# Closing the last pair of the first token block tile by tile, taking the first two tiles' scores from unsplit float32 loads, and moving the first low parts to GpSimd

## The chip, the cores and the metric

The kernel runs on one core of a Trainium2 chip. The metric is the device time of one execution in microseconds (us); three executions give the median that is compared.

## The reference, cut to what matters

Top-k attention feeds two feed-forward layers, all in float32:

```python
scores = scale * np.matmul(q, k.transpose(0, 1, 3, 2))          # (4, 8, 576, 64), scale 1/8
kth = np.partition(scores, -32, axis=-1)[..., -32:-31]
scores = np.where(scores >= kth, scores, -1e9)
attn = np.exp(scores - np.max(scores, -1, keepdims=True))
attn = attn / (np.sum(attn, -1, keepdims=True) + 1e-09)
x = np.matmul(attn, v)                                           # then (2304 tokens, 512)
h = np.maximum(x @ w_in, 0.0);   x = h * h @ w_out               # d_ff 2048
h = x @ w2_in;  out = np.maximum(0.01 * h, h) @ w2_out
```

The weights arrive as 64-bit numbers and are turned into pairs of float32 parts on the chip.

## The kernel before, in words

Queries are cut into units of 64 to 320 tokens of one batch; a unit has four head pairs (`hp`), and a unit with one head pair is a `uh`. Its queries are cut into tiles of 128 rows (two heads behind each other); two tiles make a pair (`pr`). There are 72 pairs and each pair has 16 slots of an event table: `at(slot, fn, ...)` puts a step into a slot, and the program is written out slot by slot. A scheduler then orders each engine's queue from that program with its own estimate of times; `urgent` gives a step a higher priority there, and `behind(key)` keeps an instruction after a named one. Each engine takes its own queue strictly in order, so a waiting instruction holds all behind it.

One tile goes through these steps. `load_q`, `load_k` (SP queue, DMA) bring queries and keys. `split_q`, `split_k` make a rounded high part (`split_hi`, on ACT or POOL) and a low part (a subtraction on POOL, or on DVE where `QLO_D`, `KLO_D` say so). `scores` multiplies them on PE (two products for each half of 288 keys) and ACT copies the result to `s`, scaled. DVE takes the 32 largest of a row by four MAX and three MATCH_REPLACE passes over the 576 scores, 14 passes for a pair, which are written into the first 14 slots of the pair. Then `shifts` (the difference `nb` of the 32nd and first value), `drop` and `expo_sum` (ACT: all below the 32nd go to zero, exponentials and their sum), `recip`, `pt_main` and `pt_left` (PE transposes of the probabilities `e`, copied to `PT` by ACT; also the reciprocals `rb`), `av` (product with the values) and `x_out` (DVE normalises to `xn`, ACT writes the high part `xh`, POOL or DVE the low part `xl`).

The tokens form six blocks (`BLOCKS`), the first of 512. Its attention is in the first 16 pairs (0 to 15; `first_done` is 15); only when pair 15 has given `xh` and `xl` of head pair 3 can `moe(0, 0)`, the first layer of the first block, be completed in its first products. `moe` runs 16 steps `f` for a block and layer: 12 products `h`, activation `ga`, high and low part `gh`, `gl`, 12 products `acc`. In steps met for the first time the weights are converted (`w_convert`: ACT `wc`, `att`, `wi`, `wo`; DVE bits; POOL low parts); the first two steps' weights are converted ahead by `lead_passes` and `lead_bits`. Batches 2 and 3 (`EARLY`) have their scores computed during the first 16 pairs as filler, stored to DRAM (`stage`, `sd`) and loaded later.

For pair 15 the steps stand like this, all after its 14th pass:

```python
at(z + 13, urgent(shifts), pr)
for i in range(2):
    at(z + 13, urgent(drop), pr, i)
    at(z + 13, urgent(expo_sum), pr, i)
at(z + 13, urgent(recip), pr)
for i in range(2):
    at(z + 14, urgent(pt_main), pr["t"][i])
at(z + 14, urgent(pt_left), pr)
```

When the last `x_out` of the first two units is through, `open_late` gives the SBUF of the `early` pool to the `late` one; the first `vraw` load of the later units (`load_v`, L257) goes into it, and ACT writes its high part `VT`.

## Time and profile before

| | |
|---|---|
| median of three runs | 1183.76 us (1182.36 to 1184.87) |
| the profiled execution, its own time | 1181.85 us |
| its span | 1180.1 us, 1.75 us of the time lie around it |
| PE busy | 1120.4 us (95%) |
| DVE busy | 840.8 us (71%) |
| ACT busy | 817.0 us (69%) |
| GpSimd (POOL) busy | 746.4 us (63%) |
| chain that ended last, by engine | PE 70%, ACT 10%, DVE 7%, DMA 3% |

The program has two parts. Until about 184 us DVE makes the top-k passes of the first 16 pairs while PE, ACT and POOL do the other steps and the filler; after that the feed-forward products keep PE busy to the end, with the attention of the later units beside them.

### The profile page before, as it was taken

To read this page: it belongs to the slowest core of one execution; us is meant where nothing else is said; L and a number is where in the kernel's file an instruction comes from. 1 tells how busy PE (TensorE), PEld (TensorE's weight loads), DVE (VectorE), ACT (ScalarE), POOL (GpSimd) and SP (SyncE) were. 2 spreads that over 40 slices of the span, in tenths; PEclk is the share of its full clock that TensorE was granted. 3 is DMA by queue.
4 is the path that set the end of the run, shared out by engine and by line. 5 is a ranking of instruction groups with operands and counts; after the bars stand their busy time and mean duration, and the time that the engine had idled before them with its cause. 6 is when DMAs were issued, how large, how long until landed. Compare 5 with 4: busy or idle time off the path is not lost.

```text
span 1180.1 us, 20025 instructions
## 1 busy us (share of the span) xinstructions
PE 1120.4 (95%) x6376; PEld 984.7 (83%) x6376; DVE 840.8 (71%) x1771; ACT 817.0 (69%) x1823; POOL 746.4 (63%) x960
## 2 busy tenths in 40 slices
PE   5898978899899999999999999999999999999998
PEld 4777766687678899989999998888788899999997
DVE  7999998867675669999999999989999200110011
ACT  6899997999889778877677677556866633333322
POOL 7968837899878767667898776767756543002100
PEclk9899988999999999999999999999999999999999
DMA  9768766999999588899988888667676489779974
GB/s 305 271 211 285 252 223 220 376 344 326 341 339 363 213 325 287 274 308 373 328 284 297 300 273 306 227 209 236 228 229 205 156 319 341 258 249 355 345 256 135
DMA packets 108201, 329.53 MB, mean 279 GB/s; under 512 B 17216, under 2 KB 25408, under 8 KB 104000
## 3 DMA queue, kind: packets, MB, share of 16 engines
q1 hardware_dynamic: 105472, 323.53, 79.3%
q10 hardware_dynamic: 2624, 4.72, 1.1%
q8 instruction: 52, 0.85, 0.3%
q14 instruction: 53, 0.43, 0.1%
HBM read 257.03 MB, written 71.17 MB: 278 GB/s over the span
## 4 chain that ended last, share of the span: by engine, by line
PE 70%; ACT 10%; DVE 7%; DMA 3%; issue 2%; POOL 2%; ACTq 0%; SPq 0%; POOLq 0%; DVEq 0%
PE h L653 28%; PE acc L692 15%; PE acc L690 13%; PE att L447 4%; DVE m L932 4%; PE att L350 3%; DVE w L934 3%; PE att L436 2%; ACT stage L311 1%; ACT e L333 1%; PE att L310 1%; PE sp L310 1%; ACT e L329 1%; ACT s L311 1%; DMA vraw<-in_v_dram 1%
## 5 line engine op out<-in xcount | busy, mean ns | idle before, releaser
L653 PE MATMUL h<-xh,wi 128*128 128x512 f32 (+2 forms) x1280 | 346.4, 343 | 8.8 <-ACT xh L704 3.5
L932 DVE MAX8 m<-w 128x8 f32<-128x576 f32 x432 | 311.1, 747 | 2.2
L653 PEld LDWEIGHTS h<-xh,wi 128*128 128x128 f32 x1280 | 226.1, 189 | 34.9 <-ACT ga L670 4.8
L673 POOL TENSOR_TENSOR gl<-ga,gh 128x512 fp32r<-128x512 f32 (+2 forms) x160 | 162.3, 1017 | 126.6 <-ACT gh L672 108.6
L934 DVE MATCH_REPLACE8 w<-m,w 128x576 f32<-128x576 f32 x288 | 213.0, 742 | 0.6
L653 PE MATMUL h<-xl,wi 128*128 128x512 f32 (+2 forms) x640 | 204.5, 339 | 0.0
L358 POOL TENSOR_TENSOR PTs<-whole,PTs 128x512 fp32r<-128x512 f32 x112 | 144.5, 1297 | 43.3 <-ACT whole L357 39.8
L690 PE MATMUL acc<-gh,wo 128*128 128x512 f32 (+2 forms) x768 | 157.0, 343 | 0.9 <-ACT gh L664 0.9
L692 PE MATMUL acc<-wo,gh 128*128 128x512 f32 x576 | 153.2, 397 | 0.2 <-ACT gh L672 0.2
L690 PEld LDWEIGHTS acc<-gh,wo 128*128 128x128 f32 x768 | 127.1, 190 | 13.1 <-ACT gh L664 1.7
L653 PEld LDWEIGHTS h<-xl,wi 128*128 128x128 f32 x640 | 120.3, 190 | 10.7
L329 ACT ACTIVATE e<-s,m 128x576 f32<-128x576 f32 x144 | 112.2, 782 | 24.1 <-DVE m L932 16.2
L932 DVE MAX8 m<-s 128x8 f32<-128x576 f32 x144 | 104.4, 748 | 30.3 <-ACT s L311 26.3
L673 DVE TENSOR_TENSOR gl<-ga,gh 128x384 fp32r<-128x384 f32 x32 | 17.9, 559 | 151.2 <-ACT gh L672 148.5
L670 ACT ACTIVATE ga<-h 128x512 f32<-128x512 f32 (+2 forms) x96 | 46.4, 489 | 114.1 <-PE h L653 112.1
L692 PEld LDWEIGHTS acc<-wo,gh 128*128 128x128 f32 x576 | 104.6, 188 | 20.0 <-ACT gh L672 0.4
L333 ACT ACTIVATE e<-e,nb 128x576 f32<-128x576 f32 x144 | 111.3, 778 | 4.8 <-POOL nb L323 4.7
L934 DVE MATCH_REPLACE8 w<-m,s 128x576 f32<-128x576 f32 x144 | 106.8, 743 | 0.3
L350 PE MATMUL att<-ident,e 128*128 128x128 f32 x576 | 88.5, 277 | 7.4 <-ACT e L333 6.7
L665 POOL TENSOR_TENSOR ga<-ga 128x512 f32<-128x512 f32 (+2 forms) x80 | 66.1, 828 | 44.0 <-ACT gh L664 41.6
L345 POOL TENSOR_SCALAR e<-e,rc 128x576 f32<-128x576 f32 x112 | 82.6, 748 | 11.5 <-DVE rc L341 10.9
L447 PE MATMUL att<-PTs,VT 128*128 128x256 f32 (+2 forms) x504 | 86.9, 297 | 2.0 <-ACT whole L357 1.7
(101 smaller groups left out, 2065.6 us busy)
## 6 DMA issues: line engine op xcount, KB each, us to landing
wi<-wd SPq DMA_DIRECT2D x160, 512.0 KB, 5.2
wo<-wd SPq DMA_DIRECT2D x160, 512.0 KB, 5.1
wraw<-in_w_dram SPq DMA_DIRECT2D x32, 1024.0 KB, 8.2
sd<-stage SPq DMA_DIRECT2D x76, 288.0 KB, 3.2
s<-sd SPq DMA_DIRECT2D x76, 288.0 KB, 5.0
wd<-wi SPq DMA_DIRECT2D x32, 512.0 KB, 7.4
wd<-wo SPq DMA_DIRECT2D x32, 512.0 KB, 7.3
vd<-VT SPq DMA_DIRECT2D x16, 640.0 KB, 6.3
```

Of the source, the lines that this page charges most:

```text
L329: ACT.activation(t["e"], t["s"], AF.Prelu, bias=pr["m8"][:, i, 31:32], scale=-1.0, alpha=1.0 / FAR)
L333: ACT.activation(e, e, AF.Exp, bias=pr["nb"][:, i:i + 1], scale=-FAR, accum_out=pr["sum"][:, i:i + 1])
L345: POOL.tensor_scalar(e, e, pr["rc"][:, i:i + 1], 1.0, op0=OP.mult, op1=OP.mult)
L350: PE.transpose(ps[:, j * P:(j + 1) * P], t["e"][:, j * P:(j + 1) * P], ident)
L358: POOL.tensor_tensor(pts[:, 4:8, c:c + P], whole, pts.bitcast(F)[:, 0:4, c:c + P], op=OP.subtract)
L447: PE.matmul(ps, lhsT=l, rhs=r, start=i == 0, stop=i == len(mm) - 1)
L653: PE.matmul(two[r][:, 0:n], lhsT=ws[r][:, w, c * P:(c + 1) * P], rhs=x[c][y][:, 0:n], start=cnt == mine[0], stop=cnt == mine[-1])
L673: (DVE if j >= GLD else POOL).tensor_tensor(gl[:, 0:n], a[:, 0:n], gh.bitcast(F)[:, 0:n], op=OP.subtract)
L690: PE.matmul(acc[c][:, 0:n], lhsT=wo[:, w, cs], rhs=g[:, 0:n], start=first, stop=last)
L692: PE.matmul(acc[c], lhsT=g[:, cs], rhs=wo[:, w, :], start=first, stop=last)
L932: cur["dve"] = DVE.max(out=m8[:, x, 8 * r:8 * r + 8], in_=t["s"] if r == 0 else t["w"])
L934: cur["dve"] = DVE.match_replace(out=t["w"], in_to_replace=m8[:, x, 8 * r:8 * r + 8], in_values=t["s"] if r == 0 else t["w"], imm_value=NEG)
```

## The change

Seven things change.

1. The first `uh`: its queries and keys are loaded in three DMAs each, first the 64 rows of head 0 (L288, L236), then their copy in the lower 64 partitions (L294, L242), then head 1 (L295, L243). The copy exists because the low part is made there.
2. Tiles 0 and 1 take their scores from these unsplit 64 rows as whole float32, one product for each half instead of two (L318), and are `urgent`. The split parts are still made, for tiles 2 and 3 of the same `uh`.
3. `KLO_D` and `QLO_D` are empty: the first queries' and keys' low parts go from DVE to POOL.
4. Pair 15: its passes are written one tile after the other, and `close` does everything for one tile as soon as that tile's seven passes are done. The first pass of the tiles of pair 16 stays behind the `nb` of the second close.
5. Pair 14: its closing steps are urgent, a few slots earlier, with `nb` on DVE and the sum on ACT.
6. The first two steps' weights: the sign now comes through ACT's Prelu, so DVE's second pass (L591) goes; the steps go half by half.
7. The conversion of the third step's weights starts behind the last `xh` of pair 15.

```diff
-KLO_D = ((0, 0), (0, 1))
-QLO_D = (0,)
+KLO_D = ()
+QLO_D = ()
...
+        if st["i"] == 0:
+            SP.dma_start(st["k"][0:D, 0], k[b, hp, 0:D, 0])
+            cur["k"] = st["k"]
+            return
         SP.dma_start(st["k"], k[b, hp])
+
+    def load_k_rest(b, hp, st):
+        SP.dma_start(st["k"][D:P, 0], k[b, hp, D:P, 0])
+        SP.dma_start(st["k"][:, 1], k[b, hp, :, 1])
...
+        if uh["idx"] == 0:
+            SP.dma_start(t[0:D, 0, 0:n], q[0, 0, 0:D, 0, 0:n])
+            return
...
+    def load_q_rest(uh):
+        n = uh["n"]
+        SP.dma_start(uh["q"][D:P, 0, 0:n], q[0, 0, D:P, 0, 0:n])
+        SP.dma_start(uh["q"][:, 1, 0:n], q[0, 0, :, 1, 0:n])
...
-        mm = [(x[:, h, c:c + P], kt[:, h, ks]) for h, c in t["parts"] for x in d]
+        mm = [(uh["q"][0:D, 0, t["i"] * P:t["i"] * P + P], cur["k"][0:D, 0, ks])] if t["i"] < 2 else [(x[:, h, c:c + P], kt[:, h, ks]) for h, c in t["parts"] for x in d]
...
-        on = DVE if pr["p"] == first_done else POOL
+        on = DVE if pr["p"] == first_done - 1 else POOL
...
+    def close(pr, i):
+        t, uh, m = pr["t"][i], pr["t"][i]["uh"], slice(i, i + 1)
+        if i == 0:
+            pr["nb"] = pool.tile([P, 2], F, tag="nb", name="nb", bufs=2)
+        cur["shift"] = DVE.tensor_tensor(pr["nb"][:, m], pr["m8"][:, i, 31:32], pr["m8"][:, i, 0:1], op=OP.subtract)
+        drop(pr, i)
+        expo_sum(pr, i)
+        ACT.activation(pr["sum"][:, m], pr["sum"][:, m], AF.Copy, bias=1e-9)
+        cur["recip"] = DVE.reciprocal(pr["rc"][:, m], pr["sum"][:, m])
+        pt_main(t)
+        ps = stage_psum.tile([P, 512], F, tag="sp", name="sp", bufs=SPB)
+        c, r0 = t["col"], (t["i"] - uh["ti"]) * P - uh["n"]
+        PE.transpose(ps[0:LEFT, 0:P], t["e"][:, NJ * P:S], ident)
+        ACT.activation(PT[0:64, 4, c:c + P], ps[0:64, 0:P], AF.Copy)
+        PE.transpose(ps[:, P:2 * P], pr["rc"][:, m].to_broadcast([P, P]), ident)
+        if "rb" not in uh:
+            uh["rb"] = early.tile([P, 256], F, tag="rb", name="rb", bufs=2)
+        ACT.activation(uh["rb"][D:2 * D, r0:r0 + P], ps[D:2 * D, P:2 * P], AF.Copy)
...
-            ACT.activation(b, raw[:, :, 0], AF.Copy, scale=L_SCALE, bias=L_BIAS)
+            with behind("closed") if i == 2 else ExitStack():
+                ACT.activation(b, raw[:, :, 0], AF.Copy, scale=L_SCALE, bias=L_BIAS)
...
-            ACT.activation(v, hi.bitcast(F), AF.Copy, scale=H_SCALE)
+            ACT.activation(v, hi.bitcast(F), AF.Prelu, scale=H_SCALE, alpha=2.0 ** 32)
...
-                DVE.scalar_tensor_tensor(b, vu, 0x80000000, b, op0=OP.bitwise_and, op1=OP.bitwise_or)
...
-            at(z + 13, urgent(shifts), pr)
...
+                at(z + 6 + 7 * i, urgent(close), pr, i)
...
-            z = 16 * (uh["lastA"] // 2 if hs == (0,) else uh["last"] // 2) + (15 if near else 27 if tight and apart else 30)
+            z = 16 * (uh["lastA"] // 2 if hs == (0,) else uh["last"] // 2) + (15 if near else 23 if tight and apart else 30)
...
+            if p == first_done:
+                x, r, top = i // 7, i % 7 // 2, i % 7 % 2 == 0
...
+                with behind("shift") if p == first_done + 1 and r == 0 else ExitStack():
+                    cur["dve"] = DVE.max(out=m8[:, x, 8 * r:8 * r + 8], in_=t["s"] if r == 0 else t["w"])
```

Since the scheduler orders the queues anew, they differ from the start to about the first third of PE's program; behind that (from about 420 us of the trace before) PE's queue is the same instruction for instruction.

SP's queue at the start of the program, before; `qraw_148` and `kraw_151` belong to the first `uh`, `qraw_157` to the second, `qraw_170` to the third, `qraw_224`, `qraw_226` and `kraw_230` to the filler:

```order
L279 DMA qraw_148<-in_q_dram 128x2x256
L235 DMA kraw_151<-in_k_dram 128x1152
L279 DMA qraw_157<-in_q_dram 128x2x256
L279 DMA qraw_224<-in_q_dram 128x2x256
L279 DMA qraw_226<-in_q_dram 128x2x320
L235 DMA kraw_230<-in_k_dram 128x1152
L279 DMA qraw_170<-in_q_dram 128x2x256
```

The same after (the second `uh` is now `qraw_161`, the third `qraw_174`):

```order
L288 DMA qraw_148<-in_q_dram 64x256
L294 DMA qraw_148<-in_q_dram 64x256
L290 DMA qraw_161<-in_q_dram 128x2x256
L236 DMA kraw_151<-in_k_dram 64x576
L242 DMA kraw_151<-in_k_dram 64x576
L243 DMA kraw_151<-in_k_dram 128x576
L295 DMA qraw_148<-in_q_dram 128x256
L290 DMA qraw_224<-in_q_dram 128x2x256
L290 DMA qraw_226<-in_q_dram 128x2x320
L290 DMA qraw_174<-in_q_dram 128x2x256
L239 DMA kraw_230<-in_k_dram 128x1152
```

The first keys stand fourth instead of second, the filler's keys behind the third `uh`'s queries, and that load waits for POOL's second low part of `qraw_161`.

ACT's queue at the start, before; `s0_101` and `s1_102` are the scores of tiles 0 and 1:

```order
L129 ACT_TABLE_LOAD
L129 ACTIVATE q00_77<-qraw_148 128x256 x2
L129 ACTIVATE KT_150<-kraw_151 128x576 x2
L129 ACTIVATE q01_83<-qraw_157 128x256 x2
L311 ACTIVATE s0_101<-sd_179 128x288
L311 ACTIVATE s0_101<-sd_172 128x288
L311 ACTIVATE s1_102<-sd_183 128x288
L311 ACTIVATE s1_102<-sd_187 128x288
L129 ACTIVATE q00_77<-qraw_170 128x256
```

The same after:

```order
L129 ACT_TABLE_LOAD
L129 ACTIVATE q00_77<-qraw_148 128x256
L129 ACTIVATE q01_83<-qraw_161 128x256 x2
L129 ACTIVATE KT_150<-kraw_151 128x576
L327 ACTIVATE s0_101<-sd_176 128x288
L129 ACTIVATE KT_150<-kraw_151 128x576
L129 ACTIVATE q00_77<-qraw_148 128x256
L327 ACTIVATE s0_101<-sd_182 128x288
L327 ACTIVATE s1_102<-sd_185 128x288
L129 ACTIVATE q00_77<-qraw_174 128x256
L327 ACTIVATE s1_102<-sd_188 128x288
```

The copies of the first scores are now mixed with the splits of the first `uh` and of the third; a wait for the load L294 stands ahead of the table load.

DVE's queue from the middle of the closing of pair 15 to its last low part `xl_672`, before (`m_2506` are the maxima of pair 16):

```order
L934 MATCH_REPLACE w<-m_2506,s_104 128x576
L591 SCALAR_TENSOR_TENSOR wc<-v,wc 128x512
L467 TENSOR_TENSOR xn<-att,rb 64x256
L591 SCALAR_TENSOR_TENSOR wc<-v,wc 128x512
L932 MAX m_2506<-w 128x8 x2
L934 MATCH_REPLACE w<-m_2506,w 128x576
L467 TENSOR_TENSOR xn<-att,rb 64x256
L932 MAX m_2506<-w 128x8
L472 TENSOR_TENSOR xl_672<-xn,xh_671 64x256
```

The same after (`m_2508` are the maxima of pair 16, `m_2777` those of pair 17):

```order
L502 TENSOR_TENSOR xn<-att,rb 64x256
L974 MATCH_REPLACE w<-m_2508,w 128x576
L972 MAX m_2508<-w 128x8
L972 MAX m_2508<-s_104 128x8
L974 MATCH_REPLACE w<-m_2508,s_104 128x576
L972 MAX m_2508<-w 128x8
L974 MATCH_REPLACE w<-m_2508,w 128x576
L972 MAX m_2508<-w 128x8
L972 MAX m_2777<-s_105 128x8
L502 TENSOR_TENSOR xn<-att,rb 64x256
```

Eight passes now stand between the two `xn`, three before; after them three more passes and `xl_672` follow.

ACT's queue from the last `xh` of pair 15 to the first activation `ga`, before:

```order
L468 ACTIVATE xh_671<-xn 64x256
L543 ACTIVATE wc<-wraw 128x1024
L329 ACTIVATE e_108<-s_104,m_2506 128x576
L333 ACTIVATE e_107,sum<-e_107,nb 128x576
L311 ACTIVATE s_105<-att 128x288
L129 ACTIVATE VT<-vraw 128x5x64 x2
L311 ACTIVATE s_106<-att 128x288
L333 ACTIVATE e_108,sum<-e_108,nb 128x576
L129 ACTIVATE q_77<-qraw 128x256
L311 ACTIVATE s_106<-att 128x288
L663 ACTIVATE ga<-h 128x512 x2
```

The same after:

```order
L503 ACTIVATE xh_671<-xn 64x256
L581 ACTIVATE wc<-wraw 128x1024
L590 ACTIVATE att<-wraw 128x512
L581 ACTIVATE wc<-wraw 128x1024
L327 ACTIVATE s_101<-att 128x288
L345 ACTIVATE e_108<-s_104,m_2508 128x576
L349 ACTIVATE e_107,sum<-e_107,nb 128x576
L601 ACTIVATE wi<-wc 128x512
L590 ACTIVATE att<-wraw 128x512
L349 ACTIVATE e_108,sum<-e_108,nb 128x576
L701 ACTIVATE ga<-h 128x512 x2
```

`VT` has gone behind `ga`, and the conversions of the third and fourth step's weights have come ahead of it.

## Rows read from the trace of the kernel before

**Rows 1.** The page: the span, and DVE's busy share in 40 equal slices (tenths).

```profile
span 1180.1 us, 20025 instructions
...
DVE  7999998867675669999999999989999200110011
```

**Rows 2.** Windows: us, busy time (instructions) by engine, clock, DMA share, GB/s.

```profile
190.00:200.00 10.00, 6.11 (x19) 4.59 (x19) 9.31 (x20) 9.22 (x22) 8.11 (x10) 0.71 0.67 222
200.00:240.00 40.00, 36.22 (x166) 28.74 (x165) 32.30 (x63) 36.35 (x69) 35.43 (x38) 0.99 1.00 361
240.00:300.00 60.00, 57.21 (x275) 46.97 (x276) 38.83 (x73) 55.12 (x103) 59.66 (x58) 1.00 0.95 337
```

**Rows 3.** Timeline around pair 15's closing: start, length, engine, line, operation [idle, releaser].

```profile
170.72 0.74 DVE L932 MAX8 m<-w 128x8 f32<-128x576 f32 x1
172.16 0.15 DVE L323 TENSOR_TENSOR nb<-m 128x2 f32<-128x2 f32 x1
172.23 1.28 DVE L590 SCALAR_TENSOR_TENSOR wc<-v,wc 128x512 uint32<-128x512 uint32 x2
179.70 1.12 ACT L543 ACTIVATE wc<-wraw 128x1024 uint32<-128x1024 uint32 x1
185.33 0.41 ACT L468 ACTIVATE xh<-xn 64x256 fp32r<-64x256 f32 x1
186.12 0.42 DVE L472 TENSOR_TENSOR xl<-xn,xh 64x256 fp32r<-64x256 f32 x1
190.46 0.83 ACT L129 ACTIVATE VT<-vraw 128x320 fp32r<-128x320 f32 x2 [0.31 <-DMA vraw<-in_v_dram]
192.85 1.08 ACT L663 ACTIVATE ga<-h 128x512 f32<-128x512 f32 x2
194.84 0.85 PE L310 MATMUL att<-KT,q 128*128 128x288 f32 x2 [3.66 <-ACT s L311]
195.92 3.78 PE L690 MATMUL acc<-gh,wo 128*128 128x512 f32 x8 [0.23 <-ACT gh L664]
```

**Rows 4.** The chain that ended last, in order of time: start, length, what.

```profile
244.94 2.73 PE h L653 x12
...
331.99 7.43 DMA wraw<-in_w_dram
...
581.75 2.65 DVE m L932 x4
```

**Rows 5.** Timeline of the start: columns as in rows 3.

```profile
0.73 1.28 ACT L129 ACT_TABLE_LOAD   x1 [0.73 <-PEq L995]
...
1.45 0.58 SPq L235 DMA_DIRECT2D kraw<-in_k_dram  x1
...
2.08 1.86 SPq L279 DMA_DIRECT2D qraw<-in_q_dram  x3
...
4.01 0.72 ACT L129 ACTIVATE q<-qraw 128x256 fp32r<-128x256 f32 x2 [1.99 <-DMA qraw<-in_q_dram]
...
5.63 1.26 ACT L129 ACTIVATE KT<-kraw 128x576 fp32r<-128x576 f32 x2 [0.90 <-DMA kraw<-in_k_dram]
...
7.15 1.33 PE L310 MATMUL sd<-KT,q 128*128 128x288 f32 x4 [7.15 <-DVE KT L272]
...
8.38 2.78 POOL L289 TENSOR_TENSOR q<-qraw,q 128x256 fp32r<-128x256 f32 x4
...
9.02 0.76 DVE L932 MAX8 m<-s 128x8 f32<-128x576 f32 x1 [1.25 <-ACT s L311]
...
11.22 0.69 ACT L311 ACTIVATE s<-sd 128x288 f32<-128x288 f32 x2
11.22 0.74 DVE L932 MAX8 m<-w 128x8 f32<-128x576 f32 x1
...
15.69 2.78 POOL L272 TENSOR_TENSOR KTa<-kraw,KTa 64x576 fp32r<-64x576 f32 x2
...
19.36 2.81 POOL L272 TENSOR_TENSOR KT<-kraw,KT 64x576 fp32r<-64x576 f32 x2
...
21.96 0.70 ACT L311 ACTIVATE s<-sd 128x288 f32<-128x288 f32 x2
...
23.64 0.74 DVE L932 MAX8 m<-s 128x8 f32<-128x576 f32 x1
```

**Rows 6.** DMA issues: KB each, median us from issue to landing.

```profile
qraw<-in_q_dram SPq DMA_DIRECT2D x20, 256.0 KB, 4.4
...
qraw<-in_q_dram SPq DMA_DIRECT2D x4, 64.0 KB, 2.5
```

**Rows 7.** The page's groups: busy, mean ns of one | idle before.

```profile
L333 ACT ACTIVATE e<-e,nb 128x576 f32<-128x576 f32 x144 | 111.3, 778 | 4.8 <-POOL nb L323 4.7
```

More of the change, by code (lines that the diff above doesn't have):

```diff
@@ L340, in recip @@
             POOL.tensor_scalar(pr["sum"], pr["sum"], 1e-9, 1.0, op0=OP.add, op1=OP.mult)
-        cur["recip"] = DVE.reciprocal(pr["rc"], pr["sum"])
+        DVE.reciprocal(pr["rc"], pr["sum"])
+    def close(pr, i):
[16 more added lines that the diff above has]
+        ACT.activation(uh["rb"][D:2 * D, r0:r0 + P], ps[D:2 * D, P:2 * P], AF.Copy)
     def norm(pr, i):
@@ L467, in x_out @@
             DVE.tensor_tensor(x[r, 0:n], uh["avb"][r, 0:n], uh["rb"][r, 0:n], op=OP.mult)
-        ACT.activation(xh[r, c:c + m], x[r, 0:m], AF.Copy)
+        closed = ACT.activation(xh[r, c:c + m], x[r, 0:m], AF.Copy)
         if m < n:
@@ L471, in x_out @@
         closes = uh["last"] // 2 == first_done and hs == (1,)
+        if closes:
+            cur["closed"] = closed
         (DVE if closes else POOL).tensor_tensor(xl[r, c:c + m], x[r, 0:m], xh.bitcast(F)[r, c:c + m], op=OP.subtract)
@@ L583, in lead_passes, with lead_bits @@
             ACT.activation(b, lo, AF.Copy, scale=L_SCALE, bias=L_BIAS)
-            ACT.activation(v, hi.bitcast(F), AF.Copy, scale=H_SCALE)
+            ACT.activation(v, hi.bitcast(F), AF.Prelu, scale=H_SCALE, alpha=2.0 ** 32)
             led[i].append((b, v.bitcast(U), w))
-    def lead_bits(i):
-        for b, vu, w in led.pop(i):
-            with behind("recip" if i else "shift"):
+    def lead_bits(x):
+        for i in range(2):
+            b, vu, w = led[i][x]
+            with behind("recip" if x else "shift"):
                 DVE.scalar_tensor_tensor(b, vu, 3, b, op0=OP.logical_shift_left, op1=OP.bitwise_or)
-                DVE.scalar_tensor_tensor(b, vu, 0x80000000, b, op0=OP.bitwise_and, op1=OP.bitwise_or)
             split_hi(w[:, 0, :], b.bitcast(F))
@@ L818, in topk_attention_moe_moe2_kernel @@
                 at(z - DLEAD + 2 + 5 * i, scores, t, 1)
-            at(z + 13, urgent(shifts), pr)
             for i in range(2):
-                at(z + 13, urgent(drop), pr, i)
-                at(z + 13, urgent(expo_sum), pr, i)
-            at(z + 13, urgent(recip), pr)
-            for i in range(2):
-                at(z + 14, urgent(pt_main), pr["t"][i])
-            at(z + 14, urgent(pt_left), pr)
+                at(z + 6 + 7 * i, urgent(close), pr, i)
             continue
@@ L834, in topk_attention_moe_moe2_kernel @@
             else:
-                at(z - DLEAD + 5 * i, scores, t, 0)
-                at(z - DLEAD + 2 + 5 * i, scores, t, 1)
+                mine = urgent(scores) if p == 0 else scores
+                at(z - DLEAD + 5 * i, mine, t, 0)
+                at(z - DLEAD + 2 + 5 * i, mine, t, 1)
+            soon = urgent if p == first_done - 1 else lambda fn: fn
             if i == 0:
-                at(z + 14, shifts, pr)
-            at(z + 14 + i, drop, pr, i)
-            at(z + 16 + i, expo_sum, pr, i)
+                at(z + 14, soon(shifts), pr)
+            at(z + 14 + i, soon(drop), pr, i)
+            at(z + 16 + i, soon(expo_sum), pr, i)
             if split(t["uh"]):
                 at(z + 20 + i, norm, pr, i)
-            at(max(z + 20 + 3 * i, z + 21 + i), pt_main, t)
-        at(z + 18, recip, pr)
-        at(z + 26, pt_left, pr)
+            at(z + 20 + i if p == first_done - 1 else max(z + 20 + 3 * i, z + 21 + i), soon(pt_main), t)
+        at(z + 18, soon(recip), pr)
+        at(z + 22 if p == first_done - 1 else z + 26, soon(pt_left), pr)
     rslot = [None] * len(blocks)
```

20 lines of the change are left out of this document (11 added, 9 removed).

## The prediction

> **What bounds the kernel now.** I read the page's slices first. In the first six of 40 slices (to about 177 us) DVE's digits are 7, 9, 9, 9, 9, 9 [rows 1]: there it makes the 224 passes of pairs 0 to 15. They run from 9.02 [rows 5] to the end of pair 15's last MAX, 170.72 + 0.74 = 171.46 [rows 3]: 162.4 us, 0.72 us a pass with the few other steps between. I call 171.46 T. From T the chain of waits leads through the closing of pair 15 to `moe(0, 0)`, and from about 245 us it is nearly all PE, with short stretches of DMA (331.99) and DVE (581.75) [rows 4].
>
> The timeline of the closing [rows 3] gives, counted from T: `nb` 0.7; last `xh` 13.9 (185.33); last `xl` 14.7 (186.12); `VT`, held by a DMA, 19.0 (190.46); first `ga` 21.4 (192.85); first `acc` 24.5 (195.92). PE idles 3.66 us in front of 194.84 and then makes eight `acc` products in 3.78 us, 0.47 each, where twelve `h` products later take 2.73, 0.23 each [rows 4]. In the window 190 to 200 the granted clock is 0.71, at 200 to 240 it is 0.99 [rows 2]: after the idle time PE is at the lower of its levels, 1.2 instead of 2.4 GHz. So a microsecond counts if it (a) starts DVE earlier, (b) shortens T to `ga`, or (c) fills PE's gap with products that must be made anyway.
>
> **The start (parts 1 to 3).** SP issues about 0.62 us apart (three in 1.86) and a 64 KB load lands 2.5 us after its issue, 256 KB 4.4 (median) [rows 5, 6]. The load L294 is SP's second instruction, which is issued at 1.45, and so has landed at 3.9. ACT waits for it ahead of its table load of 1.28 [rows 5], so ACT is free at 5.2 instead of 2.0. Then come, by the new queue with the row's durations (a split 0.36, a key half 0.63, a half of the scores about 0.35): 0.36 + 0.72 + 0.63 + 0.36 + 0.63 + 0.36 + 0.41 = 3.5, so the first MAX could start at 8.65 instead of 9.02. I bound it by 8.2 (L294 lands earlier) and 9.3 (it lands at 4.5). That is little, and it is not what counts: DVE has three passes on tile 0 alone and needs `s_102` for the fourth, which stood at 11.22 [rows 5]. In the new queue the second half of `s_102` is behind the split of the third `uh`'s queries; their load waits for POOL's second low part of the second `uh`. POOL makes 4 x 0.70 from 8.38 before [rows 5]; now it begins behind the first split, at 5.5, and has done three at 7.6. The first load of 256 KB takes from about 0.8 (0.62 before the 1.45 of the second) to 4.01, 3.2 us, with no other in its way; so 10.8, a split and a copy of 0.77: 11.5. The fourth pass is **0.3 us later**, not earlier; between 1.0 earlier (load under 2.5) and 1.5 later (4.4).
>
> The low parts cost POOL 2 x 0.70 + 2 x 1.39 = 4.2 us [rows 5] in front of the filler's keys; DVE loses the same pieces, but it did them while it had nothing to do, before 9.02. The second keys' low parts end at 22.17 before and feed `s_105`, used at 23.64 as the 22nd pass [rows 5]. After, I get 24.3 for the low parts' end (POOL starts earlier, so only 2.1 of the 4.2 remain), and `s_105` is now the 24th pass, at 11.5 + 20 x 0.69 = 25.3. The margin stays near 1 us: **cost 0**, and what it costs if that cover goes is rival D. PE's whole float32 products (two cold passes each) equal the split products they replace, and PE waits there anyway: 0. Four more issues on SP are 2.5 us of a queue that has free slots: 0.
>
> If the halves of a load move one after the other instead of side by side, L294 lands at 0.8 + 2 x 2.5 = 5.8, ACT is free at 7.1, the first MAX starts at 10.6 and the fourth pass at 12.7 behind three of 0.69: 1.2 later than I took. The sum below would be -1.8 instead of -3.0; the bound of 1.5 above holds it, no row of before shows a halved load, and I stay with the side-by-side value.
>
> The Trainium skill, "DMA: Bandwidth & Descriptors", section "Rules for kernel authors", states just that: two transfers to disjoint partition halves serialize, and one transfer of 128 partitions is to be used instead; by it the change's first part would cost time.
>
> **T after.** Beside the +0.3: the pass of pair 16 that stood ahead of T now stands behind it (-0.7), a second `nb` and reciprocal inside (2 x 0.15 = +0.3), gaps of less than one pass. T is unchanged, 171.5, between -1.5 and +1.5.
>
> **The closing (parts 4 to 7).** Between the last `nb` and the last `xl` the new queue of DVE has 16 passes (x 0.70 = 11.2), four steps of the weights' bits (0.64 each, half of the 1.28 in rows 3 = 2.6), two `xn` (0.42 each by the `xl` of the same shape) and a reciprocal: 14.9. So `xl` comes at T + 15.4, no earlier than T + 14.7; but the last `xn` has three passes less in front of it and the bits pass of 2.55 us (4 x 0.64, L591) is gone: 0.7 + 13 x 0.70 + 2.6 = T + 12.4, and `xh` **T + 12.9 instead of 13.9**. DVE's queue, not ACT's or PE's work on the tile, is what holds `xn`; that is why closing tile 0 seven passes early yields only one microsecond.
>
> From `xh` to `ga` ACT has, in the new order: `xh` 0.41, two `wc` 2 x 1.12 (179.70), two `att` 2 x 0.6 (half of a `wc`), `s` 0.41, a drop 0.78, `wi` 0.6, two exponentials 2 x 0.78 [rows 3, 7] = 7.2: `ga` at **T + 20.1 instead of 21.4**, 1.3 us earlier (if nothing waits for DMA: bounds 0 and 2). The load that held `VT` no longer stands in front of `ga`. In return the third step's weights are converted before it: its 12 products can be made by PE between the second step's products and the first `acc`. They are 12 x 0.23 = 2.7 us that PE needn't do later [rows 4]. PE's products of head pair 3 wait for `xl`, so of its gap I leave what I can't fill: after the 12 it has nothing from about T + 16.5 to `ga`, 3.6 us, so it idles as before and is at the lower clock behind it, as in rows 2 and 3.
>
> Against T, then: `ga` -1.3, the 12 products -2.7, and +1.0 because these twelve, and some products of later steps, run partly at the lower clock and because a step that ACT did later is now in front. Sum **-3.0** (bounds -1.5 and -4.5 with the T above). The other edits (the sum's +1e-9 on ACT, 0.2; `PT` and `rb` copied in halves; pair 14's steps, urgent) lie beside DVE's passes, which bound that stretch, so 0; without the cover each is a few tenths.
>
> **Is it kept?** From about 420 us PE's queue is the same. A lead of 3 us survives if the stretch to there isn't bound elsewhere: between 200 and 240 the DMA share is 1.00 and PE 36.2 of 40; between 240 and 300 POOL is busy 59.66 of 60 and the chain has a wait of 7.43 us for raw weights at 331.99 [rows 2, 4]. This is the weakest step. For it: the raw loads of the next steps are issued some 9 us earlier, as their buffers come free with the earlier conversion.
>
> The profiled execution took 1181.85 us, 1.9 below the median 1183.76. 1181.85 - 3.0 = 1178.85; on the median, **1180.8 us**.
>
> **The rivals.** B: the closing does what it reads like. If the scheduler's DVE queue has slack that I count as busy, the last `xh` comes at T + 10 or before, `ga` with it, and the idle 3.66 us and half of the 3.78 us behind it (1.9, products at the full clock) go as well: with rounding -6, **1178**. Against it: DVE's digits of 9 [rows 1] and 13 passes in front of `xn`.
>
> C: the lead is given back before 420 us, for POOL or the DMA decide there [rows 2]; 0, **1183.8**. For it: POOL 59.66 of 60. Against it: PE has 57.2 of 60 in that window, so POOL is not waited for at length.
>
> D, the slower side: the start starves DVE. If the third `uh`'s load takes the median 4.4 (+1.2) and POOL's 4.2 us are not absorbed, the scores `s_102` to `s_106` come late by 1.2 + 4.2 = 5.4 us in all; every microsecond in which DVE waits there moves T, and DVE has no idle time to make it up later. 5.4 less the 1.2 of the closing: +4.2, **1188**. It decides as soon as these waits exceed about 4 us in total; below that it eats the gain.
>
> That the change doesn't do what it says is part of C: DVE's queue still mixes both tiles of pair 15, so that tile 0 closes only a few passes ahead of tile 1, and `VT` behind `ga` may only move its wait.
>
> **How the numbers follow.** About 0.2%, 2.4 us, is what a measurement can tell from no change; the line lies at 1181.4. My forecast has a chance of 0.45 with its own range of 1179.3 to 1182.3 (faster 0.28, same 0.17). B 0.20, all faster. C 0.20 (same 0.18, slower 0.02). D 0.15 (slower 0.12, same 0.03). Together faster 0.48, same 0.38, slower 0.14. The range reaches from 1176.0 (B, 2 us more) to 1186.0, which leaves out the worse half of D and the far end of B.
>
> **What would show it.** First MAX near 8.7 and the fourth pass near 11.5; no idle time of DVE over 1 us between 12 and 35 us (D if there is). T near 171.5. Last `xh` about T + 13 and `ga` about T + 20 (B: `xh` by T + 10, PE without a gap over 1 us). Twelve more `h` products in front of the first `acc`, and a granted clock in that window again well below 1. From 420 us on PE's instructions shifted by one constant, 3 us; if the shift is 3 at 200 and 0 at 420, it is C. The forecast is wrong in kind if T itself moves by more than 1.5 us or if a new wait on DMA shows between `xh` and `ga`.

## The result and the profile after

The changed kernel takes 1196.16 us (median of six runs, 1191.96 to 1197.46) against 1183.8 of the kernel before: ratio 1.0104 (95% interval 1.0086 to 1.0121), 12.4 us slower. The prediction was 1180.8, range 1176.0 to 1186.0. The profiled execution took 1197.46 us; its page answers to [rows 1]:

```profile
span 1195.6 us, 20042 instructions
...
DVE  6997999776676567999999999999999300110011
```

DVE's fourth slice (about 90 to 120 us) has dropped from 9 to 7, the first from 7 to 6: DVE waits in the stretch where its passes set the time. The timeline of ACT, PE and DVE at the start (start, length, engine, line, operation, [idle before, releaser]) answers to [rows 5]:

```profile
3.69 1.28 ACT L129 ACT_TABLE_LOAD   x1 [3.69 <-DMA qraw<-in_q_dram]
6.18 4.30 PE L326 MATMUL sd<-kraw,qraw 64*128 64x288 f32 x8 [6.18 <-DMA kraw<-in_k_dram]
6.95 0.68 ACT L129 ACTIVATE KT<-kraw 128x576 fp32r<-128x576 f32 x1 [0.70 <-DMA kraw<-in_k_dram]
9.14 0.76 DVE L972 MAX8 m<-s 128x8 f32<-128x576 f32 x1 [9.14 <-ACT s L327]
12.68 0.42 ACT L129 ACTIVATE q<-qraw 128x256 fp32r<-128x256 f32 x1 [2.83 <-DMA qraw<-in_q_dram]
13.43 0.76 DVE L972 MAX8 m<-s 128x8 f32<-128x576 f32 x1 [1.88 <-ACT s L327]
```

The first pass is at 9.14 (9.02 before), the fourth at 13.43 (11.22 before). The fourth pass waits for a copy of `s_102` behind ACT's split of the third `uh`'s queries, and that split waits for their load. That is the chain of the prediction, but 1.9 us later than its 11.5.

DVE's waits between 20 us and the end of pair 15's passes, before (first fence) and after (second; what waits, for what, us in total, times, longest):

```profile
DVE m L932 <- ACT s L311: 1.1, 2, 0.8
DVE rc L341 <- POOL sum L340: 0.7, 3, 0.3
DVE m L932 <- ACT q L129: 0.6, 1, 0.6
DVE m L932 <- POOL nb L323: 0.5, 1, 0.5
```

```profile
DVE m L972 <- ACT s L327: 4.5, 3, 3.2
DVE m L972 <- POOL nb L339: 2.2, 2, 1.3
DVE rc L357 <- POOL sum L356: 1.1, 1, 1.1
DVE xn L502 <- ACT rb L436: 0.9, 2, 0.6
```

That is 2.9 us before and 8.7 after; those after all lie beyond 80 us. The last MAX of pair 15 ends at 181.12 (180.38 + 0.74) instead of 171.46 [rows 3]: 9.7 later, of which 2.2 is the fourth pass, 5.8 the growth of these waits, and 1.7 I can't assign (0.64 of it may be the `nb` of pair 14, which now takes that long on DVE at 174.44). The first `ga` follows at 204.10, 23.0 us behind that MAX (21.4 before):

```profile
180.38 0.74 DVE L972 MAX8 m<-w 128x8 f32<-128x576 f32 x1
183.89 0.76 DVE L972 MAX8 m<-s 128x8 f32<-128x576 f32 x1 [1.73 <-ACT s L327]
197.50 0.41 ACT L503 ACTIVATE xh<-xn 64x256 fp32r<-64x256 f32 x1
204.10 1.06 ACT L701 ACTIVATE ga<-h 128x512 f32<-128x512 f32 x2
204.73 0.50 PE L691 MATMUL h<-xh,wi 128*128 128x512 f32 x1 [2.27 <-ACT ga L701]
209.44 2.02 PE L728 MATMUL acc<-gh,wo 128*128 128x512 f32 x8
```

PE's idle time around `ga` is 2.27 instead of 3.66. The third step's 12 products do stand before the first `acc`, and the first eight `acc` take 2.02 us instead of the 3.78 before.

`ga` is 11.3 us late, the end of the span 15.5 (1195.6 against 1180.1). To see where the rest goes I counted ACT's copies `gh` (the high parts made from `ga`) from the program's end and compared their starts with the same copy before. The copy that stood at 238.2 us is 10.4 late, the one at 278.3 13.2, at 326.7 15.1, at 430.7 15.2, at 654.8 15.3, and the last one (1170.7) 15.8. So another 4 us are lost between about 240 and 330 us, and from there the delay is nearly constant. The first 40 us behind `ga` are not it: counted from each kernel's own `ga` they are the same before (first line) and after (second), in PE's busy time (34.19 and 34.10 us) and in the granted clock (0.91 and 0.91):

```profile
192.85:232.85 40.00, 34.19 (x142) 26.79 (x143) 35.70 (x70) 36.10 (x70) 35.01 (x36) 0.91 0.97 348
204.10:244.10 40.00, 34.10 (x143) 27.07 (x144) 29.88 (x59) 34.74 (x69) 36.92 (x39) 0.91 0.90 326
```

Behind that, the chain that ended last differs. Before, it runs from 245 to 299 us mostly through PE's products, and between 200 and 360 us through one load of raw weights (331.99, 7.43 us [rows 4]). In the changed kernel it runs through four, at 213.06, 347.10 and, where the 4 us are lost, at

```profile
290.10 7.97 DMA wraw<-in_w_dram
300.88 8.77 DMA wraw<-in_w_dram
```

That these loads make the 4 us is read from the chain; no run changes them alone, and e1, which is not late, has two such loads on its chain there (196.14 and 256.24).

Where the first of DVE's waits beyond 80 us comes from shows in POOL's and PE's rows. The first rows are of the kernel before, the second of the changed one, at the same place of the program:

```profile
79.91 1.06 PE L310 MATMUL sp<-KTa,q 128*128 128x288 f32 x6
80.81 2.52 PE L436 MATMUL att<-PT,VN 128*128 128x256 f32 x10
```

```profile
82.48 0.79 PE L326 MATMUL sp<-KTa,q 128*128 128x288 f32 x4
83.11 1.89 PE L471 MATMUL att<-PT,VN 128*128 128x256 f32 x8
...
85.78 0.53 PE L326 MATMUL sp<-KTa,q 128*128 128x288 f32 x2
86.27 0.46 POOL L131 TENSOR_SCALAR q<-qraw 128x320 fp32r<-128x320 f32 x1 [3.28 <-PE sp L326]
...
96.55 2.76 POOL L280 TENSOR_TENSOR KT<-kraw,KT 64x576 fp32r<-64x576 f32 x2
99.39 0.20 POOL L339 TENSOR_TENSOR nb<-m 128x2 f32<-128x2 f32 x1
99.62 1.42 DVE L972 MAX8 m<-s 128x8 f32<-128x576 f32 x2 [1.32 <-POOL nb L339]
```

Before, all six products of a filler step stand ahead of the ten products `att`; now two of them stand behind. POOL's next split waits 3.28 us for those two (its buffer is free only then), does the filler's keys and the direct keys behind that, comes late with `nb`, and DVE's next MAX waits for `nb`. The longest wait, 3.17 us, ends with ACT's copy of the second half of a tile's scores:

```profile
111.99 0.69 PE L326 MATMUL sd<-KT,q 128*128 128x288 f32 x4
113.64 1.01 ACT L327 ACTIVATE stage<-sp 128x288 f32<-128x288 f32 x3
114.80 0.81 ACT L345 ACTIVATE e<-s,m 128x576 f32<-128x576 f32 x1
115.47 0.44 ACT L327 ACTIVATE s<-sd 128x288 f32<-128x288 f32 x1
115.95 0.76 DVE L972 MAX8 m<-s 128x8 f32<-128x576 f32 x1 [3.17 <-ACT s L327]
```

PE has the products at 112.68, but three copies of the filler's scores (`stage`) and a drop stand ahead of that copy in ACT's queue. Both chains are read from the rows; the experiments below move whole queues and don't single any wait out.

### The profile page after: what moved, and what is told of

The parts are those of the page before. It is cut to its first block, busy times and chain, and to the rows that moved or that the text cites. A ratio compares the mean times of both kernels' runs of the same rounds, so it can differ in the third digit from the quotient of the medians.

```text
span 1195.6 us, 20042 instructions
## 1 busy us (share of the span) xinstructions
PE 1128.1 (94%) x6376; PEld 989.9 (83%) x6376; DVE 839.5 (70%) x1766; ACT 817.7 (68%) x1827; POOL 751.7 (63%) x962
## 4 chain that ended last, share of the span: by engine, by line
PE 64%; ACT 8%; DVE 5%; DMA 4%; issue 2%; POOL 1%; ACTq 0%; SPq 0%; DVEq 0%; POOLq 0%
PE h L691 28%; PE acc L730 15%; PE acc L728 11%; PE att L482 4%; PE att L385 3%; DMA wraw<-in_w_dram 3%; DVE m L972 2%; DVE w L974 2%; PE att L326 1%; ACT wc L581 1%; ACT e L349 1%; ACT att L590 1%; PE att L400 1%; ACT e L345 1%; DMA wi<-wd 1%
## 5 line engine op out<-in xcount | busy, mean ns | idle before, releaser
L728 PEld LDWEIGHTS acc<-gh,wo 128*128 128x128 f32 x768 | 126.5, 189 | 12.1 <-ACT gh L702 1.0
L730 PEld LDWEIGHTS acc<-wo,gh 128*128 128x128 f32 x576 | 104.8, 188 | 20.2 <-ACT gh L710 0.4
```

The source lines that it names most:

```text
L728: PE.matmul(acc[c][:, 0:n], lhsT=wo[:, w, cs], rhs=g[:, 0:n], start=first, stop=last)
L730: PE.matmul(acc[c], lhsT=g[:, cs], rhs=wo[:, w, :], start=first, stop=last)
```

## The experiments

Eighteen kernels and the changed one were compared with the one before; the table gives ratios of medians with their 95% intervals. Times against the kernel before are the ratio less one, times 1183.8; their intervals are 1.8 to 3.7 us to either side.

| kernel | low parts | order of the queues | ratio | us |
|---|---|---|---|---|
| changed kernel | POOL | its own | 1.0104 (1.0086 to 1.0121) | +12.3 |
| e1 closing only | DVE | its own | 0.9970 (0.9952 to 0.9987) | -3.6 |
| e2 start only | POOL | its own | 1.0142 (1.0122 to 1.0162) | +16.8 |
| e3 low parts DVE | DVE | its own | 1.0030 (1.0014 to 1.0046) | +3.6 |
| e4 whole loads, POOL | POOL | its own | 1.0093 (1.0066 to 1.0121) | +11.0 |
| e5 keys on POOL | keys POOL | its own | 1.0009 (0.9990 to 1.0028) | +1.1 |
| e6 queries on POOL | queries POOL | its own | 1.0048 (1.0030 to 1.0066) | +5.7 |
| e7 filler later | POOL | its own | 1.0104 (1.0074 to 1.0135) | +12.3 |
| e8 no hold | DVE | its own | 0.9999 (0.9984 to 1.0014) | -0.1 |
| e9 | POOL | that of e1 | 0.9999 (0.9982 to 1.0016) | -0.1 |
| e10 | DVE | that of e4 | 1.0136 (1.0112 to 1.0160) | +16.1 |
| e11 | POOL, all parts | that of e1 | 0.9989 (0.9973 to 1.0005) | -1.3 |
| e12 | POOL, all parts | e1, start by hand | 1.0048 (1.0027 to 1.0070) | +5.7 |
| e14 | DVE | e1, behind the closing e4 | 1.0120 (1.0089 to 1.0151) | +14.2 |
| e15 | DVE | e4, behind the closing e1 | 1.0039 (1.0021 to 1.0057) | +4.6 |
| e16 | DVE | e4 up to pair 6, then e1 | 0.9987 (0.9968 to 1.0006) | -1.5 |
| e17 | POOL, all parts | e1, start by hand | 1.0051 (1.0035 to 1.0068) | +6.0 |
| e18 | POOL, all parts | own, behind the closing e1 | 1.0091 (1.0062 to 1.0119) | +10.8 |
| e19 | POOL, all parts | e1, start by hand | 1.0025 (1.0009 to 1.0041) | +3.0 |

**Which part costs it: e1 to e4.** e1 takes parts 1 to 3 back:

```diff
-KLO_D = ()
-QLO_D = ()
+KLO_D = ((0, 0), (0, 1))
+QLO_D = (0,)
...
-        if st["i"] == 0:
+        if False:
...
-        if uh["idx"] == 0:
+        if False:
...
-        mm = [(uh["q"][0:D, 0, t["i"] * P:t["i"] * P + P], cur["k"][0:D, 0, ks])] if t["i"] < 2 else [(x[:, h, c:c + P], kt[:, h, ks]) for h, c in t["parts"] for x in d]
+        mm = [(x[:, h, c:c + P], kt[:, h, ks]) for h, c in t["parts"] for x in d]
...
-            if i == 0:
-                at(z0 + 1, load_k_rest, b, hp, st)
...
-        if i == 0:
-            at(z - 62, load_q_rest, uh)
...
-                mine = urgent(scores) if p == 0 else scores
+                mine = scores
```

> The changed kernel with its start put back as before (whole loads, split scores for tiles 0 and 1, first low parts on DVE); parts 4 to 7 stay. Theory S (the start holds DVE back, first by the load of the third uh's queries and then by stalls between 80 and 160 us that follow from it): the fourth pass is back near 11.2, pair 15's last MAX ends near 171.5 instead of 181.1, and the time is 1181 to 1185. Theory C (the closing and the urgent steps of pair 14 and 15 cost it): T stays within 2 us of 181, the time 1193 to 1197. Theory Q (every new order of the scheduler has its own stalls in the filler): T anywhere between, with other stalls than those at 99, 112 and 116 us.

e2 is the kernel before with parts 1 to 3 alone, e3 the changed kernel with only the lines `KLO_D` and `QLO_D` of that diff, e4 the changed kernel with all of it but these two lines.

> The kernel before with parts 1 to 3 alone (three loads, whole float32 scores of tiles 0 and 1, low parts on GpSimd). S: fourth pass near 13.4, T near 181, time 1190 to 1197. C: T near 171.5 to 174, time 1182 to 1187. Q: T elsewhere, stalls at other places.

> The changed kernel with part 3 alone undone: the first queries' and keys' low parts are on DVE again. If POOL's added work is the cause (it delays the release of the third uh's buffer and all of POOL's later splits): the fourth pass comes at 11.5 or before, T within 2 us of 172, time 1181 to 1186. If the three loads and the mixed order of ACT are the cause: the fourth pass stays above 12.5 and T above 178.

> The changed kernel with parts 1 and 2 undone, part 3 kept: whole loads and split scores, but the first low parts on GpSimd. If POOL's added work is the cause: first scores wait for POOL's low parts (first MAX about 10 to 12), T above 178, time above 1190. If the loads and ACT's order are the cause: T within 3 us of 172 plus the delay of the first MAX, time 1182 to 1188.

The closing alone is 3.6 us faster, the start alone 16.8 slower. Of the start, either half by itself costs: the loads and whole products 7.2 (e3 less e1), the low parts on POOL 14.6 (e4 less e1), both together 15.9. That they don't add was the first sign that neither is a plain cost. The traces of e2 and e4 show, further below, that most of e2's loss and nearly half of e4's is made behind 430 us, so these differences are not the price of the start's work.

**Is it POOL's time: e5 to e8.** e5 and e6 set only one of the two names in e1 to `()`. e7 is the changed kernel with one line changed (first cut), e8 is e1 with one line changed (second):

```diff
-FILL = (2, 222)
+FILL = (10, 222)
```

```diff
-            with behind("closed") if i == 2 else ExitStack():
+            with ExitStack():
```

> The closing alone (first kernel of this study), with the first keys' low parts (2 x 1.4 us) on GpSimd, the first queries' still on DVE. Theory P (POOL's added time decides, in proportion): two thirds of the +15 between the closing alone and the closing with both on GpSimd, +10, 1190 to 1193. Theory K (POOL is held behind the first keys, which come late, so the keys alone do it): 1193 to 1198. Theory Q (the scheduler's new order has its own stalls, the size of POOL's work does not matter): 1181 to 1200, not in proportion.

> The closing alone, with the first queries' low part (2 x 0.7 us) on GpSimd, the keys' on DVE. P: one third, +5, 1185 to 1188. K: within 1.5 us of the closing alone, 1180 to 1183. Q: not in proportion; a large loss from 1.4 us on POOL, above 1190, would be Q.

> The changed kernel with the filler (scores of batches 2 and 3) starting eight slots later (about 5.6 us of DVE's passes), so that POOL has the 4.2 us of first low parts behind it before the filler's splits want it. P: the collision at the start is gone, the last MAX of pair 15 ends 6 us or more earlier than in the changed kernel, time 1181 to 1188. Q: other stalls, 1190 to 1200.

> The closing alone without its part 7 (the third step's conversions no longer wait for the last xh of pair 15). If the hold moves ga earlier by keeping those conversions out of the way of the closing (the prediction has it at about 1 of the 3 us): 1181 to 1184, last xh 1 to 3 us later, T to ga above 23. If the gain of the closing alone sits in DVE before T (its last MAX was 2.0 us earlier than before): within 1 us of the closing alone.

2.8 us of work moved to POOL cost 4.7 us over e1, and 1.4 us cost 9.3: the loss is not in proportion to POOL's time, against theory P. e7's total doesn't speak against P as it seems to. In its trace pair 15's last MAX ends at 175.32, 5.8 us earlier than in the changed kernel, and the `gh` copy of 430.7 us is 5.5 late instead of 15.2; the rest of its loss is made behind that, where its order is new again. Nor does e8 price part 7: its total is 3.5 us above e1's, but its trace is 6.8 us ahead of the kernel before at 430.7 (e1's is 0.7 ahead) and loses that later. Whether POOL's time is the cause is left to the next three.

**The cross: e9 to e11.** The scheduler's order can be held. Each instruction keeps its number as long as the program is written out the same; these kernels carry a list of numbers for each engine and tie each instruction behind the one that stands ahead of it there. Up to about 162 us, e1's order on PE, DVE, ACT and POOL is that of the kernel before, instruction for instruction:

```diff
+def keep_order(tc, nc):
+    import base64, json, zlib
+    rows = json.loads(zlib.decompress(base64.b85decode(ORDER)))
+    by = {i.name: i for i in nc.cur_bb.bb.instructions}
+    for queue in rows.values():
+        names = ["I-%d" % n for n in queue if "I-%d" % n in by]
+        for a, b in zip(names, names[1:]):
+            tc.add_manual_dep(by[b], a, mybir.DependencyInfo(
+                mybir.DependencyClass.NoSync, mybir.DependencyReason.DATA), reason="order")
...
         topk_attention_moe_moe2_kernel(tc, *args)
+        keep_order(tc, nc)
```

> The closing alone, with the first low parts (4.2 us) on GpSimd, but every engine's queue held in the order that the closing alone has (only the four low parts stand at the head of POOL's queue instead of DVE's). Left to the scheduler the same program took 1196. Theory O (the scheduler's new order makes the loss, not the 4.2 us on POOL): 1180 to 1184, no wait of DVE over 1 us between 20 and 160 us. Theory P (POOL's 4.2 us themselves): 1190 to 1197 in this order too. In between (1185 to 1189): both.

> The other half of the cross: low parts on DVE as before, POOL free of them, but every queue in the order that the scheduler made for low parts on POOL with whole loads (the one that took 1196). O: the loss stays, 1191 to 1197, with DVE waiting at the same instructions near 100 to 160 us. P: 1180 to 1184.

> The whole changed kernel, all seven parts, with its own start of each queue (loads, splits, first scores, low parts), and behind that the order of the closing alone; the third uh's split stands behind the second half of tile 1's scores. O: 1180 to 1186, the fourth pass near 11 to 12, T within 2 us of 171. P: 1190 to 1197.

This settles that the order is the cause. With e1's order, low parts on DVE or POOL give -3.6 and -0.1; with e4's order +16.1 and +11.0. The order makes 11 to 20 us, and theory P, POOL's time as the cause, falls. The place of the low parts makes 3.5 in favour of DVE in e1's order, and 5.1 in favour of POOL in e4's. The whole changed kernel, all seven parts, takes 1181.6 us in e1's order. No kernel was held in the order that its own scheduler run had made, so what the ties cost by themselves isn't shown; that e9 and e11, with every queue tied, are no slower than the kernel before leaves them little. DVE's waits between 20 and 170 us, first of e9, then of e11:

```profile
DVE m L968 <- ACT s L327: 0.7, 2, 0.4
DVE m L968 <- POOL nb L339: 0.5, 2, 0.3
DVE rc L357 <- POOL sum L356: 0.3, 2, 0.2
```

```profile
DVE m L972 <- ACT s L327: 0.6, 2, 0.4
DVE m L972 <- POOL nb L339: 0.5, 1, 0.5
DVE m L972 <- ACT q L129: 0.4, 1, 0.4
DVE rc L357 <- POOL sum L356: 0.4, 2, 0.2
```

That is 1.5 and 1.9 us, where the changed kernel in its own order has 8.7. At the start, e9 shows what the 4.2 us on POOL do when nothing else moves: the second keys' low parts end at 23.60 (22.17 before [rows 5]), and the one wait that follows is 0.28 us:

```profile
20.78 2.82 POOL L280 TENSOR_TENSOR KT<-kraw,KT 64x576 fp32r<-64x576 f32 x2
24.50 0.76 DVE L968 MAX8 m<-s 128x8 f32<-128x576 f32 x1 [0.28 <-ACT s L327]
```

**Where the order loses it: e14 to e16 and e18.** These kernels have the program up to a point in one order and the rest in the other. One engine's queue of one order among the others' queues of the other order was not tried.

> Program of the closing alone (low parts on DVE). Queues in the closing-alone order up to the nb of pair 15's second close, behind that the order that the scheduler made with low parts on POOL. Whole-program values: 1181 in the first order, 1198 in the second. If the loss is made in the opening: 1180 to 1184. If the order behind the closing makes its own loss (in the trace of the second order the shift against before grows from 12 to 20 us between 530 and 655 us): 1187 to 1191, with that growth there and T near 170.

> The other way round: the second order up to pair 15's second close, the first behind it. Opening alone: 1190 to 1198. Both halves make a part: 1187 to 1191, T 6 to 7 us late and the shift constant from 430 us on.

> The second order only up to the first pass of pair 6 (about 65 us), the first behind it. If the start and its first 65 us make DVE late for good: 1186 to 1190. If the damage is done by the order between 65 and 170 us (where DVE's waits stand in the trace): 1180 to 1184.

> The changed kernel itself, all its work: its own queues up to the nb of pair 15's second close, behind that the order of the closing alone. Bounds: 1196 with its own order throughout, 1181.6 with the other order throughout. Its trace was 9.7 us late at the last MAX of pair 15 and 15.2 us late from 430 us on. If that 9.7 is made in the opening and the other 5 by the order behind it: about 1190 to 1192. If the order behind it gives the opening's delay back: 1184 to 1188. If the opening carries all: 1194 to 1197.

e16: e4's order of the first 65 us costs nothing that stands clear of the intervals (-1.5 against e1's -3.6). e15: its opening as a whole costs 8.2 us over e1, so most of the opening's loss in e4's order is made between 65 and 170 us, where DVE's waits are, not at the start. e14: the order behind the closing costs even more in that pair, 17.8. The changed kernel differs there, since its PE queue is that of before from 420 us on: with e1's order behind the closing, e18, it stays 10.8 slower, so its opening carries 12.1 of the 13.6 us that lie between its own order and e1's. The shift of the `gh` copies against the kernel before, counted from the end (us), shows it in single executions:

| copy at (before) | changed | e1 | e9 | e10 | e11 | e14 | e15 | e16 | e18 |
|---|---|---|---|---|---|---|---|---|---|
| 430.7 | +15.2 | -0.7 | +0.8 | +12.3 | +0.5 | +7.4 | +5.7 | -0.4 | +12.2 |
| 654.8 | +15.3 | -1.6 | -0.1 | +20.2 | -0.5 | +16.3 | +4.8 | -1.4 | +11.4 |
| 1170.7 | +15.8 | -1.4 | -0.2 | +20.5 | -0.2 | +16.7 | +5.2 | -1.2 | +11.4 |

The same for the kernels whose order the scheduler made:

| copy at (before) | e2 | e3 | e4 | e5 | e6 | e7 | e8 |
|---|---|---|---|---|---|---|---|
| 430.7 | +4.0 | +8.2 | +8.7 | +1.4 | +2.1 | +5.5 | -6.8 |
| 654.8 | +18.3 | +8.2 | +16.2 | +1.5 | +6.8 | +12.8 | -0.1 |
| 1170.7 | +19.0 | +9.0 | +16.3 | +1.9 | +8.6 | +13.1 | +1.9 |

So a new order loses time in two places. In the changed kernel, e1, e3 and e5, and in those held in e1's order behind the closing, PE's queue is that of the kernel before again from about 400 to 500 us on, and the shift differs by at most 1.0 us between the three copies. In e2, e4, e6, e7, e10 and e14 PE's queue differs up to about 1010 us, in e8 up to about 950. There 6 to 15 us are lost behind 430.7, far from the start and from the closing. Nor does a late last MAX set the time alone: in e2 it ends at 180.90, as late as in the changed kernel, yet at 430.7 e2 is only 4.0 us late.

In e18 the longest of DVE's waits in the changed kernel are back at their places, the first longer (1.08 there), the second of the same length (3.17 there):

```profile
113.18 0.17 DVE L357 RECIPROCAL rc<-sum 128x2 f32<-128x2 f32 x1 [2.89 <-POOL sum L356]
117.90 0.76 DVE L972 MAX8 m<-s 128x8 f32<-128x576 f32 x1 [3.16 <-ACT s L327]
```

**Can the earlier scores gain anything: e12, e17, e19.** These have all parts and e1's order, but the start in an order by hand. The first rows of e19's ACT queue stand below. In e12 all four copies of the first two scores stand ahead of the splits; e17 has them as here, and puts the products and copies of `s_105` ahead of the filler's; e19 does so with `s_106` and with pair 0's drops too:

```order
L327 ACT_TABLE_LOAD
L327 ACTIVATE s0_101<-sd_176 128x288
L129 ACTIVATE KT_150<-kraw_151 128x576
L327 ACTIVATE s0_101<-sd_182 128x288
L129 ACTIVATE q00_77<-qraw_148 128x256
L327 ACTIVATE s1_102<-sd_185 128x288
L327 ACTIVATE s1_102<-sd_188 128x288
```

> As the last, but with a start in an order written by hand: head 0's queries and keys are loaded first, ACT copies the four halves of the first scores before any split, the low parts that tiles 2 and 3 need come first on POOL, the second keys' low parts stand ahead of the filler's. If the idea of the unsplit scores holds, the first MAX starts near 5.7 to 7 instead of 9.0; O: the time is 1177 to 1183 (the other engines keep up with part of the 2 to 3 us). P or a wait for s_103 to s_105 that eats it: 1184 to 1192.

> The start by hand once more, with the two faults that its trace showed mended: head 1's splits stand between the four copies of the first scores (these come 0.96 us apart, as fast as PE makes the whole float32 products), and the products and copies of tile s_105 stand ahead of the filler's first products, for which they waited 7.7 us. Expected: first MAX near 7.4, the sixth pass near 11.3, T 1.5 to 3 us earlier than in the changed kernel in the old order; 1177 to 1181. If POOL's later start binds (s_105 or s_106 waits over 1 us): 1181 to 1186.

> The start by hand once more: the last trace had its first MAX at 7.10 and then a wait of 7.9 us at 30 us for ACT's drops of pair 0, which stood behind the filler's copies, and s_106's copies stood there too. Now the drops, s_105 and s_106 stand ahead of the filler's first copies, and pair 0's nb ahead of the filler's low parts. If the start's gain of about 2 us carries: 1178 to 1181, T near 170. If the filler, started later, holds something else up: another wait of DVE, 1182 to 1190.

The first MAX comes at 7.28, 7.10 and 7.10, up to 1.9 us earlier than before, and each time a wait elsewhere takes it back: 7.66 us for `s_105` at 32.50 in e12, then those in e17 (first fence) and e19 (second):

```profile
30.11 0.76 DVE L972 MAX8 m<-s 128x8 f32<-128x576 f32 x1 [7.88 <-ACT e L345]
```

```profile
24.21 0.76 DVE L972 MAX8 m<-s 128x8 f32<-128x576 f32 x1 [1.98 <-ACT e L345]
31.10 0.17 DVE L357 RECIPROCAL rc<-sum 128x2 f32<-128x2 f32 x1 [4.75 <-POOL sum L356]
```

The gain that I expected came in none of the three: each order by hand left or opened another wait. Whether the unsplit scores can pay stays open. The only kernel that is faster than the one before clear of its interval is e1, 1181.08 us (ratio 0.9970), the closing without the start.

## Why the prediction was wrong, point by point

**The step that failed is "T is unchanged, 171.5, between -1.5 and +1.5"**, and in it the silence on the 150 us between the start and the closing. I compared the orders at the start and at the seam, priced those, and let the rest stand as if the queues between were the old ones, although the section on the change says that they differ. T was 9.7 us later. In the profiled executions, the shift of 15.2 us at 430.7 is made of 9.7 up to T, 1.6 from T to `ga` (forecast: -1.3) and 4.0 behind `ga` (forecast: -2.7 for the products and +1.0, a term for which I had no row). The runs put in the step's place: in a held order the start's work costs about what I summed (e11 less e1, +2.3; e9 less e1, +3.5), and the order that the scheduler makes around it costs 13.6 (changed kernel less e11), 12.1 of them by the opening (e18 less e11).

**The start.** First MAX 8.65 forecast, 9.14 measured; fourth pass 11.5 forecast with bounds of 10.2 and 12.7, 13.43 measured. The first MAX is late by a wait that my sum left out: ACT's split of the first keys waits 0.70 us for their load (at 6.95). The fourth pass is late by the load of the third `uh`: it had not landed 4.5 us after its latest possible issue (SP's three loads of that line occupy 5.04 to 8.14, ACT's split is released at 12.68), where I had 3.2, and 4.4 as the bound. The whole float32 products, which I priced like the split ones as "two cold passes each", were mis-sized too: 4.30 us for eight instructions against 2.66 for eight of the split ones (two times the 1.33 of [rows 5]). That did not set either pass here, as the copies of `s` that they fed stood behind other work of ACT or ahead of the late split. The low parts on POOL were right: their end was forecast at 24.3 and is 24.27 (21.47 + 2.80).

**Halved loads.** L294 was issued at 1.39, and by 3.69, when their wait released ACT's table load, both halves had landed: at most 2.3 us after its issue, and not at the 5.8 of the other reading. The Trainium skill, "DMA: Bandwidth & Descriptors", section "Rules for kernel authors", says that two such halves serialize. The trace's records of the DMA packets agree in the order (the first half's lie between 2.1 and 2.7 us, the second's between 2.7 and 3.3), though the issues, 0.65 us apart, would give the same; but what follows one behind the other is half a microsecond of packets, not the 2.5 us from issue to landing that I doubled. No run here loads both halves as one.

**The closing** was forecast at -3.0, and alone it gives -3.6 by ratio (-1.5 to -5.7), -2.8 by medians. The sum agreed, its terms did not, so the agreement is luck. The rows of e1:

```profile
168.67 0.76 DVE L968 MAX8 m<-w 128x8 f32<-128x576 f32 x1
183.24 0.43 DVE L502 TENSOR_TENSOR xn<-att,rb 64x256 f32<-64x256 f32 x1 [1.06 <-ACT rb L376]
183.90 0.42 ACT L503 ACTIVATE xh<-xn 64x256 fp32r<-64x256 f32 x1
191.81 1.06 ACT L701 ACTIVATE ga<-h 128x512 f32<-128x512 f32 x2
```

T is 169.43, 2.0 us earlier than before, where I had 0. The pass of pair 16 that now stands behind T takes its 0.7 and a wait of 0.75 (at 170.04 before) with it. The kernel before also waited 0.59 and 0.53 us at 54 and 94 us, where e1's queues are still the same as its own, so this part is a difference between executions: e14, the same program in the same order up to the closing, has T at 170.73. From T the last `xh` takes 14.5, not 12.9 (13.9 before), for `xn` waits 1.06 us for ACT's copy `rb`: here DVE's queue wasn't what held it, as I had said. It wasn't in the kernel before either, where the last `xn` (184.87) waits 0.91 us for the same copy. And `xh` to `ga` is 7.9, not 7.2, with `VT` again in front of `ga` in e1's order. So `ga` is 1.0 us earlier (I had 1.3 without the gain in T). In the changed kernel the last `xh` comes 16.4 us after T (197.50), 3.5 later than forecast; 1.73 of that is DVE's wait at 183.89 for a copy of `s`, which my count of passes did not have. There `xn` starts without a wait, and `xh` to `ga` takes 6.6.

**The rivals.** D had the sign and the place where it starts (chance of slower: 0.14), but not the mechanism: it wanted `s_102` to `s_106` late by 5.4 us in the first 30 us and POOL's 4.2 us as the cause. The waits in the first 30 us were 1.88 beyond the first MAX, those that decide come after 80 us, and e9 shows POOL's 4.2 us nearly harmless. C, a lead lost between 200 and 420 us, holds in sign: another 4 us went there in the changed kernel, with loads of raw weights on the chain, which I had expected earlier, not later. The rival that I lacked was "the new order of the queues, taken as a whole, is worse", which neither side of my sum contained. Its size could not be read from the trace of before, but its possibility could: I knew that one third of PE's queue had changed, and that the passes have no idle time to make anything up.

## What to carry to other kernels

Where a scheduler orders the queues, an edit at the start is two edits: the work it moves, and a new order of everything that the scheduler decides later; here the second weighed 13.6 us against the 2.3 of the work in the old order. It may also lose time far from the edit: e6, with 1.4 us of work moved at the start, lost 6 of its 9 us behind 430 us. So ask of each trace where the delay grows before you put its total down to the edit. Hold the order while you measure an edit, by tying each instruction behind its predecessor in the old queue, and let go of it only if the free order is faster. In a stretch where one engine has no idle time, look for chains through the in-order queues that end at it: here two filler products behind others on PE, a split on POOL 3.28 us late, `nb`, and then 1.32 us of DVE.
